# Output weight loaded ahead of the second chunk's v, first q norms as one-column matmuls, first A^T W in landing order

## Chip, core, metric

One core of one Trainium2 chip. The metric is the device time of one launch in microseconds (us). PE is the matmul engine, ACT the scalar and DVE the vector engine; POOL issues the loads. An eviction is the scaled copy of a result out of PSUM.

## The reference

```python
# q, k, v: (4, 6144, 256); w1, w2, w3: (256, 768); w_out: (768, 256)
qn = q / (norm(q, axis=1) + 1e-6);  kn = k / (norm(k, axis=1) + 1e-6)
a = softmax(kn^T @ qn / tau)              # per batch, 256 x 256
x = (v @ a).reshape(24576, 256)
h = max(max(x @ w1, x @ w2), x @ w3)      # 24576 x 768
out = h @ w_out
```

The kernel never forms x. It computes A^T-times-weight products (`aw`, 256 x 768, three of them) per batch and multiplies v by them, so that one 512-row chunk of v costs 36 h matmuls and 24 output products. A product below is a matmul of `aw`; `et` is the exponential of the softmax.

## The kernel before, where the change touches it

Loads run on one queue in this order: k, q (in pieces of 8, 8, 8, 8, 4, 4, 4, 2, 2 row groups), v of chunk 0, nine pieces of w, v of chunk 1. The output weight follows only after chunk 1's v is transposed.

```python
    load_v(0)
    for fp in range(d_ff // FT):
        load_w(fp)                       # w1, w2, w3, 256 columns each
    load_v(1)
    ...
    def gram(b):                         # first batch only
        ...                              # k.k, diagonal into dkm
        for tp in range(NG // 2):        # pairs of row groups, double-row fp8
            for j in range(CC):
                PE.matmul(ps[j][:, 0:C], lhsT=qt[:, tsl, jsl], rhs=kt[:, tsl, :], ...)          # q.k
                PE.matmul(ps[j][:, C:C + P], lhsT=qt[:, tsl, jsl], rhs=qt[:, tsl, jsl], ...)    # q.q
    def softmax_t(ps, rkb):
        for j in range(CC):              # the diagonal of q.q holds the squared norms
            DVE.tensor_tensor_reduce(out=scr, in0=ps[j][:, C:C + P], in1=ident, ..., accum_out=n2q[:, j:j + 1])
        ...                              # Ln, Exp, scaled exp into et
    def aw_first(et, aw):
        products(0, (0, 1)); sums(0); sums(1)
        DVE.reciprocal(out=rinv, in_=rs_ps[:, 0:CC])
        products(1, (0, 1))
        for j in range(CC):
            products(j, (2,))
        # then six evictions, ACT and DVE in turn, scaled by rinv
    ...
    # after chunk 1's v has been transposed:
    hold_loads(1)
    POOL.dma_start(out=wo_sb, in_=moe_w_out.rearrange("(fc p) d -> p fc d", p=P))
    load_v(2)
```

`h_block` computes one 128-row block of h for a chunk: two matmuls for each of the three weights, a copy of the first bank on ACT and two maxima on DVE. Six PSUM banks rotate under products and h matmuls, two under grams, transposes, row sums and outputs.

## Time and profile before

| | before |
|---|---|
| time, median of 4 runs | 573.33 us (573.17 to 573.77) |
| span of the profiled run | 571.9 us |
| PE busy | 97% |
| last q piece reaches PE | 33.87 us |
| first h matmul | 37.73 us |
| next products (end of the first h block) | 39.02 us |
| first output product | 51.07 us |

The lines are in the prediction below. Three things help to read them. A timeline line of several instructions gives the start of the first and the length up to the end of the last; a matmul's own length (0.27 for a 256-wide one) contains its drain, so the step between starts, not the length, is what it costs. The idle time in brackets is that of the engine just before. And a transfer in the chain of waits costs only what PE waited at its end.

### The profile page before, as it was taken

How to read it: one execution, taken by the hardware profiler on the slowest of the kernel's cores; microseconds unless marked ns; L12 is line 12 of the kernel's file. 1: busy time of each engine (PE TensorE's matmuls, PEld its weight loads, DVE VectorE, ACT ScalarE, POOL GpSimd, SP SyncE). 2: the span in 40 equal slices, each digit the busy share in tenths (PEclk: the TensorE clock that was granted, in tenths of full speed). 3: DMA queues.
4: the chain of work that ended last, by engine and by line, in shares of the span. 5: the costliest groups of instructions: out<-in, count | busy, mean ns of one | idle time of the engine just before them, and what ended most of it. 6: DMA issues, size and time to landing. Idle time of an engine off the chain costs nothing.

```text
span 571.9 us, 9438 instructions
## 1 busy us (share of the span) xinstructions
PE 552.9 (97%) x3344; PEld 329.1 (58%) x3344; DVE 415.9 (73%) x658; ACT 309.1 (54%) x540; POOL 233.3 (41%) x237
## 2 busy tenths in 40 slices
PE   3799999999999999999999999999999999999997
PEld 2665555555755555555575555555575555555566
DVE  0048777777887777777767777777768778778775
ACT  1044567767464576776535467767635444444443
POOL 2442357776460078776560048777750000000000
PEclk9999999999999999999999999999999999999999
DMA  9997999895479268975279339985437333132112
GB/s 143 106 147 121 132 238 138 158 133 107 111 83 171 70 109 157 135 149 107 57 133 149 97 79 141 147 143 99 122 81 160 75 77 108 56 104 64 56 55 76
DMA packets 76960, 65.64 MB, mean 115 GB/s; under 512 B 52464, under 2 KB 62576, under 8 KB 76784
## 3 DMA queue, kind: packets, MB, share of 16 engines
q0 software_dynamic: 19072, 26.48, 39.1%
q1 hardware_dynamic: 57696, 38.41, 24.1%
q8 instruction: 26, 0.43, 0.3%
q14 instruction: 22, 0.18, 0.1%
q10 hardware_dynamic: 144, 0.13, 0.1%
HBM read 78.64 MB, written 25.17 MB: 182 GB/s over the span
## 4 chain that ended last, share of the span: by engine, by line
PE 90%; DMA 6%; issue 2%; POOL 1%; DVE 0%; POOLq 0%
PE h_ps L378 64%; PE o_ps L398 22%; DMA v_sb<-in_v_dram 3%; PE gram L249 3%; PE ew_ps L300 2%; DMA q_sb<-in_q_dram 1%; DMA wo_sb<-in_moe_w_out_dram 1%; DMA vt_sb<-v_sb 1%; POOL k_sb L99 0%; PE o_ps L423 0%; POOL w_sb L135 0%; POOL q_sb L102 0%; DVE o_sb L450 0%; POOL ident masks.py:199 0%; PE rs_ps L288 0%
## 5 line engine op out<-in xcount | busy, mean ns | idle before, releaser
L378 PE MATMUL h_ps<-vt_sb,aw_sb 128*128 128x512 bf16 (+1 forms) x1764 | 406.6, 375 | 0.1
L378 PEld LDWEIGHTS <-aw_sb 128*128 128x128 bf16 x1764 | 171.7, 98 | 161.7 <-DVE aw_sb L306 2.4
L383 DVE TENSOR_TENSOR s_mx<-h_ps,s_mx 128x512 bf16<-128x512 f32 (+1 forms) x294 | 198.8, 676 | 82.2 <-ACT s_mx L382 82.0
L382 ACT ACTIVATE s_mx<-h_ps 128x512 bf16<-128x512 f32 (+1 forms) x294 | 172.3, 586 | 124.3 <-PE h_ps L378 123.4
L384 DVE TENSOR_TENSOR ht_sb<-h_ps,s_mx 128x512 bf16<-128x512 f32 (+1 forms) x294 | 200.2, 681 | 30.6
L208 POOL TENSOR_TENSOR acc<-acc,sq 128x768 f32<-128x768 f32 x88 | 144.3, 1649 | 69.3 <-ACT sq L200 53.1
L398 PE MATMUL o_ps<-wo_sb,ht_sb 128*128 128x256 bf16 x1128 | 153.8, 273 | 0.1
L398 PEld LDWEIGHTS <-ht_sb 128*128 128x128 bf16 x1128 | 110.4, 98 | 52.2 <-issue 0.3
L401 ACT ACTIVATE o_sb<-o_ps 128x512 f32<-128x512 f32 x94 | 56.1, 597 | 83.9 <-PE o_ps L398 83.9
L110 POOL DMA_DIRECT2D v_sb<-in_v_dram x48 | 27.8, 584 | 37.4 <-DMA vt_sb<-v_sb 35.2
L200 ACT ACTIVATE sq<-q_sb 128x768 bf16<-128x768 fp8e4 x48 | 40.5, 844 | 0.0
L200 ACT ACTIVATE sq<-k_sb 128x768 bf16<-128x768 fp8e4 x48 | 40.1, 835 | 0.0
L205 POOL CAST acc<-sq 128x768 f32<-128x768 bf16 x6 | 4.9, 821 | 65.7 <-ACT sq L200 65.7
L102 POOL DMA_DIRECT2D q_sb<-in_q_dram x33 | 18.4, 565 | 4.1 <-DMA v_sb<-in_v_dram 3.1
L168 PE MATMUL kk<-k_sb 128*128 128x256 fp8e4 x48 | 7.5, 338 | 12.3 <-DVE k_sb L154 6.5
L99 POOL DMA_DIRECT2D k_sb<-in_k_dram x29 | 16.1, 557 | 2.9 <-issue 1.1
L249 PE MATMUL gram<-k_sb,q_sb 128*128 128x512 fp8e4 x144 | 16.8, 276 | 0.0
L249 PEld LDWEIGHTS <-q_sb 128*128 128x256 fp8e4 x144 | 15.9, 136 | 0.6
L303 ACT ACTIVATE aw_sb<-ew_ps,rinv 128x384 bf16<-128x384 f32 (+1 forms) x24 | 13.1, 554 | 5.7 <-PE ew_ps L300 4.8
L221 POOL PARTITION_ALL_REDUCE tot<-acc x6 | 10.9, 1858 | 11.9 <-DVE s_mx L383 6.0
L300 PE MATMUL ew_ps<-w_sb,et 128*128 128x384 bf16 (+1 forms) x96 | 15.6, 313 | 0.0
L168 PEld LDWEIGHTS <-k_sb 128*128 128x256 fp8e4 x48 | 6.4, 182 | 13.2 <-DMA k_sb<-in_k_dram 6.7
(64 smaller groups left out, 116.5 us busy)
## 6 DMA issues: line engine op xcount, KB each, us to landing
out_dram<-o_sb SPq DMA_DIRECT2D x41, 512.0 KB, 2.9
v_sb<-in_v_dram POOLq DMA_DIRECT2D x48, 256.0 KB, 4.4
k_sb<-in_k_dram POOLq DMA_DIRECT2D x24, 192.0 KB, 5.9
q_sb<-in_q_dram POOLq DMA_DIRECT2D x24, 192.0 KB, 7.3
out_dram<-o_sb SPq DMA_DIRECT2D x13, 256.0 KB, 2.0
k_sb<-in_k_dram POOLq DMA_DIRECT2D x5, 256.0 KB, 11.2
w_sb<-in_moe_w_dram POOLq DMA_DIRECT2D x9, 128.0 KB, 5.7
kf<-in_k_dram SPq DMA_DIRECT2D x1, 1024.0 KB, 5.0
```

Source lines behind the costliest of these rows:

```text
L102: POOL.dma_start(out=qk[b][0][:, g0:g0 + w, :], in_=q_r[b][:, g0:g0 + w, :])
L110: POOL.dma_start(out=t, in_=v_r[gi // NCH, gi % NCH])
L200: ACT.activation(out=sq, in_=src, func=AF.Square)
L208: POOL.tensor_tensor(out=acc, in0=acc, in1=sq, op=ALU.add)
L249: PE.matmul(g[:, j * C:(j + 1) * C], lhsT=qt[:, tsl, j * P:(j + 1) * P], rhs=kt[:, tsl, :], start=(tp == 0 and j == 0), stop=(tp == NG // ...
L300: PE.matmul(ew[:, :w], lhsT=et[:, j, ic * P:(ic + 1) * P], rhs=w_sb[m][:, j, fsl], start=(j == 0), stop=(j == CC - 1))
L378: PE.matmul(t.rearrange("p (t n) -> p t n", n=P), lhsT=aw[m][:, ic, fsl], rhs=vt[:, tsl, ic, :], start=(ic == 0), stop=(ic == CC - 1))
L382: ACT.activation(out=s_mx, in_=hp[0], func=AF.Copy)
L383: DVE.tensor_tensor(out=s_mx, in0=hp[1], in1=s_mx, op=ALU.max)
L384: DVE.tensor_tensor(out=ht, in0=hp[2], in1=s_mx, op=ALU.max)
L398: PE.matmul(st["ps"][:, half], lhsT=ht[:, fc, t * P:(t + 1) * P], rhs=wo_sb[:, fc, :], start=(fc == 0), stop=(fc == FC - 1))
L401: ACT.activation(out=st["o"][:, t - 1:t + 1, :].rearrange("p t d -> p (t d)"), in_=st["ps"], func=AF.Copy)
```

## The change

Three parts, all in the first 52 us. The output weight's load goes ahead of chunk 1's v, so that the first output product need not wait. The q norms of the first batch come from squares on ACT and DVE, summed over partitions by matmuls against a column of ones, instead of q.q matmuls and diagonal reductions. The first products follow the landing order of the weights, with each row sum ahead of them; the third weight's products move into the first h block; the transposed v of chunk 0 goes to two banks, six of its eight blocks to be copied by DVE and two by ACT, where each copied four.

```diff
     for fp in range(d_ff // FT):
         load_w(fp)
+    wo_sb = consts.tile([P, FC, d_model], BF16, name="wo_sb")
+    POOL.dma_start(out=wo_sb, in_=moe_w_out.rearrange("(fc p) d -> p fc d", p=P))
     load_v(1)
 ...
+        def squares(g0, w):
+            ACT.activation(out=a[:, 0:h, :], in_=ra, func=AF.Square)
+            DVE.tensor_tensor(out=d[:, 0:h, :], in0=rd, in1=rd, op=ALU.mult)
+        def columns(rows, first=False, last=False):
+            for n, (t, r) in enumerate(rows):
+                for j in range(CC):
+                    PE.matmul(nq[:, j:j + 1], lhsT=t[:, r, j * P:(j + 1) * P], rhs=ones_c, ...)
 ...
-        products(0, (0, 1))
+        weight(0)
         sums(0)
+        products(0, 0)
         sums(1)
         DVE.reciprocal(out=rinv, in_=rs_ps[:, 0:CC])
-        products(1, (0, 1))
+        products(1, 0)
+        weight(1)
         for j in range(CC):
-            products(j, (2,))
+            products(j, 1)
 ...
+        def third(between):
+            weight(2)
+            for j in range(CC):
+                products(j, 2)
+            evacuate(2 * CC + 1, DVE)
+            between()
+            evacuate(2 * CC, ACT)
 ...
+    def h_block_first(aw, third):
+        matmuls(0, range(CC))
+        third(lambda: ACT.activation(out=s_mx, in_=hp[0], func=AF.Copy))
+        matmuls(1, range(CC))
+        matmuls(2, reversed(range(CC)))
 ...
-    for i in range(6):
-        PE.matmul(warm_ps, lhsT=ident, rhs=warm, start=(i == 0), stop=(i == 5))
+    for i in range(2):
+        PE.matmul(warm_ps, lhsT=ident, rhs=warm, start=(i == 0), stop=(i == 1))
```

More of the change, by code (lines that the diff above doesn't have):

```diff
@@ L75 @@
     sq_pool = ctx.enter_context(tc.tile_pool(name="sq", bufs=4))
+    sqq_pool = ctx.enter_context(tc.tile_pool(name="sqq", bufs=3))
     sm = ctx.enter_context(tc.tile_pool(name="sm", bufs=2))
@@ L118 @@
     SP.dma_start(out=kf, in_=k_r[0][:, 0:HEAD, :])
-    for load, widths in ((load_k, [8] * 5), (load_q, [8] * 4 + [4, 4, 4, 2, 2])):
+    QW = [8] * 4 + [4, 4, 4, 2, 2]
+    for load, widths in ((load_k, [8] * 5), (load_q, QW)):
         g0 = HEAD if load is load_k else 0
@@ L139 @@
         load_w(fp)
+    wo_sb = consts.tile([P, FC, d_model], BF16, name="wo_sb")
+    POOL.dma_start(out=wo_sb, in_=moe_w_out.rearrange("(fc p) d -> p fc d", p=P))
     load_v(1)
-    wo_sb = consts.tile([P, FC, d_model], BF16, name="wo_sb")
     ACT.preload_act_table_set("natural_log_exp_and_others")
@@ L157, with gram_first @@
     neg_ln_tau = -math.log(float(tau)) if float(tau) != 1.0 else 0.0
-    def gram(b):
-        qt, kt = qk[b]
+    def gram_first():
+        qt, kt = qk[0]
         kk = htile("kk")
@@ L173, in gram @@
             DVE.tensor_tensor(out=dkm[:, jsl], in0=kk[:, jsl], in1=ident, op=ALU.mult)
-        ps = [xtile(f"gram{j}") for j in range(CC)]
-        for tp in range(NG // 2):
-            tsl = slice(2 * tp, 2 * tp + 2)
-            last = tp == NG // 2 - 1
-            for j in range(CC):
-                jsl = slice(j * P, (j + 1) * P)
-                PE.matmul(ps[j][:, 0:C], lhsT=qt[:, tsl, jsl], rhs=kt[:, tsl, :],
-                          start=(tp == 0), stop=last, perf_mode=DR, skip_group_check=True)
-                PE.matmul(ps[j][:, C:C + P], lhsT=qt[:, tsl, jsl], rhs=qt[:, tsl, jsl],
-                          start=False, stop=last, perf_mode=DR, skip_group_check=True)
-            if tp == 11:
+        g = xtile("gram")
+        nq = htile("nq")
+        def squares(g0, w):
+            h = w // 2
+            a = sqq_pool.tile([P, QW[0] // 2, C], BF16, name="sqa")
+            d = sqq_pool.tile([P, QW[0] // 2, C], BF16, name="sqd")
+            ra, rd = qt[:, g0:g0 + h, :], qt[:, g0 + h:g0 + w, :]
+            ACT.activation(out=a[:, 0:h, :], in_=ra, func=AF.Square)
+            DVE.tensor_tensor(out=d[:, 0:h, :], in0=rd, in1=rd, op=ALU.mult)
+            return [(t, r) for t in (a, d) for r in range(h)]
+        def columns(rows, first=False, last=False):
+            for n, (t, r) in enumerate(rows):
+                for j in range(CC):
+                    PE.matmul(nq[:, j:j + 1], lhsT=t[:, r, j * P:(j + 1) * P], rhs=ones_c,
+                              start=(first and n == 0 and j == 0), stop=(last and n == len(rows) - 1),
+                              skip_group_check=True)
+        g0 = 0
+        rows = None
+        for i, w in enumerate(QW):
+            if rows:
+                columns(rows, first=(i == 1))
+            for tp in range(g0 // 2, (g0 + w) // 2):
+                tsl = slice(2 * tp, 2 * tp + 2)
+                for j in range(CC):
+                    PE.matmul(g[:, j * C:(j + 1) * C], lhsT=qt[:, tsl, j * P:(j + 1) * P], rhs=kt[:, tsl, :],
+                              start=(tp == 0 and j == 0), stop=(tp == NG // 2 - 1), perf_mode=DR,
+                              skip_group_check=True)
+            rows = squares(g0, w)
+            g0 += w
+            if i == 2:
                 kb_ps = htile("kb_ps")
@@ L190, in gram @@
                 ACT.activation(out=rkb, in_=lnk, func=AF.Exp, scale=-0.5)
-        return ps, rkb
+        columns(rows, last=True)
+        return [g[:, j * C:(j + 1) * C] for j in range(CC)], rkb, nq[:, 0:CC]
     SQW = 3
@@ L265, in exp_t, with softmax_first @@
         return et
-    def softmax_t(ps, rkb):
-        n2q = sm.tile([P, CC], FP32, name="n2q")
-        scr = sm.tile([P, P], FP32, name="scr")
-        for j in range(CC):
-            DVE.tensor_tensor_reduce(out=scr, in0=ps[j][:, C:C + P], in1=ident, scale=1.0, scalar=0.0,
-                                     op0=ALU.mult, op1=ALU.add, accum_out=n2q[:, j:j + 1])
+    def softmax_first(gs, rkb, n2q):
         lnq = sm.tile([P, CC], FP32, name="lnq")
@@ L276, in softmax_t @@
         ACT.activation(out=rq, in_=lnq, func=AF.Exp, scale=-0.5, bias=neg_ln_tau)
-        return exp_t(scaled([ps[j][:, 0:C] for j in range(CC)], rkb), rq)
+        return exp_t(scaled(gs, rkb), rq)
     def alloc_aw():
@@ L313, in aw_first, with weight @@
         rs_ps = xtile("rs_ps")
-        parts = [(m, ic, htile("ew_ps")) for m in range(3) for ic in range(CC)]
+        parts = []
+        def weight(m):
+            parts.extend((m, ic, htile("ew_ps")) for ic in range(CC))
         def sums(j):
@@ L319, in sums, with products, evacuate @@
                           start=(ic == 0 and j == 0), stop=(j == CC - 1), skip_group_check=True)
-        def products(j, ms):
+        def products(j, of):
             for m, ic, ew in parts:
-                if m in ms:
+                if m == of:
                     PE.matmul(ew[:, :FT], lhsT=et[:, j, ic * P:(ic + 1) * P], rhs=w_sb[m][:, j, 0:FT],
                               start=(j == 0), stop=(j == CC - 1))
-        products(0, (0, 1))
+        def evacuate(n, engine):
+            m, ic, ew = parts[n]
+            dst, src, r = aw[m][:, ic, 0:FT], ew[:, :FT], rinv[:, ic:ic + 1]
+            if engine is ACT:
+                ACT.activation(out=dst, in_=src, func=AF.Copy, scale=r)
+            else:
+                DVE.tensor_scalar_mul(out=dst, in0=src, scalar1=r)
+        weight(0)
         sums(0)
+        products(0, 0)
         sums(1)
         DVE.reciprocal(out=rinv, in_=rs_ps[:, 0:CC])
-        products(1, (0, 1))
+        products(1, 0)
+        weight(1)
         for j in range(CC):
-            products(j, (2,))
-        for n, (m, ic, ew) in enumerate(parts):
-            if n % 2 == 0:
-                ACT.activation(out=aw[m][:, ic, 0:FT], in_=ew[:, :FT], func=AF.Copy, scale=rinv[:, ic:ic + 1])
-            else:
-                DVE.tensor_scalar_mul(out=aw[m][:, ic, 0:FT], in0=ew[:, :FT], scalar1=rinv[:, ic:ic + 1])
-        return rinv
+            products(j, 1)
+        for m in range(2):
+            evacuate(CC * m, ACT)
+            evacuate(CC * m + 1, DVE)
+        def third(between):
+            weight(2)
+            for j in range(CC):
+                products(j, 2)
+            evacuate(2 * CC + 1, DVE)
+            between()
+            evacuate(2 * CC, ACT)
+        return rinv, third
     vts = {}
@@ L358, in v_transpose_pe @@
         vt = vt_tile(gi)
-        vt_ps = xtile("vt_ps", cols=TPC * C, dtype=BF16)
-        for i in range(TPC * CC):
-            PE.matmul(vt_ps[:, i * P:(i + 1) * P], lhsT=v_sb[:, i * P:(i + 1) * P], rhs=ident,
-                      is_transpose=True, start=(i == 0), stop=(i == CC * TPC - 1))
-        half = TPC * CC // 2
-        ps = vt_ps.rearrange("p (i n) -> p i n", n=P)
-        DVE.tensor_copy(out=vt[:, half:, :], in_=ps[:, half:, :])
-        ACT.activation(out=vt[:, :half, :], in_=ps[:, :half, :], func=AF.Copy)
+        n = TPC * CC
+        cut = 6
+        banks = [xtile("vt_ps", cols=TPC * C, dtype=BF16), ps_h.tile([P, TPC * C], BF16, tag="h", name="vt_ps2")]
+        for b, (lo, hi) in enumerate(((0, cut), (cut, n))):
+            for i in range(lo, hi):
+                PE.matmul(banks[b][:, i * P:(i + 1) * P], lhsT=v_sb[:, i * P:(i + 1) * P], rhs=ident,
+                          is_transpose=True, start=(i == lo), stop=(i == hi - 1))
+        pa, pb = (t.rearrange("p (i n) -> p i n", n=P) for t in banks)
+        DVE.tensor_copy(out=vt[:, 0:cut, :], in_=pa[:, 0:cut, :])
+        ACT.activation(out=vt[:, cut:n, :], in_=pb[:, cut:n, :], func=AF.Copy)
     def h_block(gi, aw, fc, tsl=slice(0, TPC)):
@@ L382, in h_block, with matmuls @@
         ACT.activation(out=s_mx, in_=hp[0], func=AF.Copy)
+        DVE.tensor_tensor(out=s_mx, in0=hp[1], in1=s_mx, op=ALU.max)
+        DVE.tensor_tensor(out=ht, in0=hp[2], in1=s_mx, op=ALU.max)
+    def h_block_first(aw, third):
+        vt = vts[0]
+        hp = []
+        def matmuls(m, ics):
+            t = htile(f"h_ps{m}")
+            for n, ic in enumerate(ics):
+                PE.matmul(t.rearrange("p (t n) -> p t n", n=P), lhsT=aw[m][:, ic, 0:P], rhs=vt[:, :, ic, :],
+                          start=(n == 0), stop=(n == CC - 1))
+            hp.append(t)
+        s_mx = mx_pool.tile([P, CHUNK], BF16, name="s_mx")
+        ht = hts[0][:, 0, :]
+        matmuls(0, range(CC))
+        third(lambda: ACT.activation(out=s_mx, in_=hp[0], func=AF.Copy))
+        matmuls(1, range(CC))
+        matmuls(2, reversed(range(CC)))
         DVE.tensor_tensor(out=s_mx, in0=hp[1], in1=s_mx, op=ALU.max)
@@ L452, in last_chunk @@
         SP.dma_start(out=dst[:, HT + 1, :], in_=o_sb[:, HT + 1, :])
-    ps = gram(0)
+    first = gram_first()
     warm_ps = htile("warm_ps")
-    for i in range(6):
-        PE.matmul(warm_ps, lhsT=ident, rhs=warm, start=(i == 0), stop=(i == 5))
-    et = softmax_t(*ps)
+    for i in range(2):
+        PE.matmul(warm_ps, lhsT=ident, rhs=warm, start=(i == 0), stop=(i == 1))
+    et = softmax_first(*first)
     v_transpose_pe(0)
     aw = alloc_aw()
-    rinv = aw_first(et, aw)
+    rinv, third = aw_first(et, aw)
     v_transpose(1)
@@ L471 @@
     hold_loads(1)
-    POOL.dma_start(out=wo_sb, in_=moe_w_out.rearrange("(fc p) d -> p fc d", p=P))
     load_v(2)
@@ L532 @@
             for fc in range(FC):
-                h_block(gi, aw, fc)
+                if gi == 0 and fc == 0:
+                    h_block_first(aw, third)
+                else:
+                    h_block(gi, aw, fc)
                 for f in gaps[fc]:
```

## The prediction

> **What bounds the kernel now.** I read the page's busy shares and slices first, then the chain of waits, then the timeline of the first 52 us, because all three parts of the change lie there.
>
> ```profile
> PE 552.9 (97%) x3344; PEld 329.1 (58%) x3344; DVE 415.9 (73%) x658; ACT 309.1 (54%) x540; POOL 233.3 (41%) x237
> PE   3799999999999999999999999999999999999997
> PE 90%; DMA 6%; issue 2%; POOL 1%; DVE 0%; POOLq 0%
> ```
>
> PE is full in every slice but the first two and the last. So a change in the head pays only by the amount by which the dense stream of matmuls starts earlier, or by holes that it fills. The chain of waits, cut to 0 to 75 us (start, length, what):
>
> ```profile
> 16.32 7.09 DMA q_sb<-in_q_dram
> 23.69 11.37 DMA v_sb<-in_v_dram
> 36.74 5.64 DMA v_sb<-in_v_dram
> 42.39 2.89 DMA vt_sb<-v_sb
> 45.57 5.45 DMA wo_sb<-in_moe_w_out_dram
> 51.07 0.82 PE o_ps L398 x6
> ```
>
> Read back, the first output product waits for the output weight, whose load was issued only at 45.57, after the second chunk's v was loaded and transposed. But the chain overstates that load: 5.45 us of it run beside dense PE work. How long PE itself waited comes from the timeline (start, length, engine, line, instruction, idle before):
>
> ```profile
> 33.87 0.32 PE L180 MATMUL gram<-k_sb,q_sb 128*128 128x512 fp8e4 x1 [0.15 <-DMA q_sb<-in_q_dram]
> 34.26 1.47 PE L458 MATMUL warm_ps<-warm,ident 128*128 128x512 bf16 x6
> 34.29 0.29 DVE L271 CUSTOM_DVE_ANT_0 scr<-gram,ident 128x128 f32<-128x128 f32 x1 [13.89 <-PE gram L182]
> 35.07 0.20 ACT L275 ACTIVATE lnq<-n2q 128x2 f32<-128x2 f32 x1 [6.22 <-DVE n2q L271]
> 35.54 0.91 ACT L264 ACTIVATE et<-e_in,rq 128x256 bf16<-128x256 f32 x2
> 35.56 0.61 PE L361 MATMUL vt_ps<-ident,v_sb 128*128 128x128 bf16 x8
> 36.10 0.70 PE L324 MATMUL ew_ps<-w_sb,et 128*128 128x256 bf16 x4
> 36.63 0.24 PE L318 MATMUL rs_ps<-ones_c,et 128*128 128x1 bf16 x4
> 36.67 0.60 ACT L366 ACTIVATE vt_sb<-vt_ps 128x512 bf16<-128x512 bf16 x1 [0.23 <-DVE vt_sb L365]
> 37.18 1.20 ACT L336 ACTIVATE aw_sb<-ew_ps,rinv 128x256 bf16<-128x256 f32 x3
> 37.73 1.46 PE L378 MATMUL h_ps<-vt_sb,aw_sb 128*128 128x512 bf16 x6
> 39.02 1.47 PE L300 MATMUL ew_ps<-w_sb,et 128*128 128x256 bf16 x12
> ...
> 44.37 6.63 PE L378 MATMUL h_ps<-vt_sb,aw_sb 128*128 128x512 bf16 x30
> ```
>
> Until 33.87 the load of q sets the pace. Then comes the chain of the first softmax (reduce, Ln, Exp, scaled exp), and from 36.10, when the first half of et is there, PE is nearly dense. Check: six h matmuls take 1.29 us in the chain, so 0.216 each; a 256-wide product takes 0.109 ((1.47 - 0.27)/11). From 36.10 up to the first output product the work is 36 products (3.92), 4 row sums (0.10) and 48 h matmuls (10.37), together 14.39 us. The 30 h matmuls from 44.37 run out at 44.37 + 30 x 0.216 = 50.85; the output product starts at 51.07. So PE lost 0.22 us to the output weight, and 50.85 - 36.10 - 14.39 = 0.36 us in small holes. That is all the slack there is after 36.10. The rest of any gain has to come from starting before 36.10.
>
> **What the Trainium skill says.** (1) "TensorE: Matmul & The Clock Gate", section "Wait — 56ns, not 53.3ns?": starts of small matmuls are never closer than about 25 ns. The trace agrees: four 1-column row sums take 0.24 us, that is 0.165 for one and three steps of 0.025. (2) Same page, "Part 1: The HAM clock gate": PE begins at half rate and is released by about 3.4 us of sustained work. The trace agrees in kind: in the gram stage the starts of a q.k and a q.q matmul lay 0.32 us apart from 21.0 on and 0.168 from 24.9 on, after 3.9 us without a hole. The k stage before it, busy 1.25 of each 2.45 us, never got the faster clock. (3) "PSUM — Partial Sum Buffer", "Terms": two engines may not use the same bank and quadrant at once. The 0.23 us that ACT's copy of vt waits for DVE's copy of the same bank agrees. (4) "SBUF — State Buffer", "SBUF: two separate sides": a DVE instruction with two SBUF inputs contends with a GpSimd instruction that reads SBUF. The new squares on DVE are such; nothing in this trace shows whether they hold up the issue of loads.
>
> **The change part by part.**
>
> *Norms as columns.* Removed: 48 q.q matmuls, two DVE diagonal reductions and four of the six warm-up matmuls. Added: for each of nine pieces of q a square on ACT and one on DVE, and 96 one-column matmuls (96 x 0.025 = 2.4 us, against 48 x 0.056 = 2.7 removed). Up to the last piece all this is beside the load: a piece of 8 groups comes every 2.45 us and costs at full clock 8 x 0.109 + 16 x 0.025 = 1.27 us of PE, and about 1.1 to 1.2 us on ACT and DVE (estimate from ACT's 768-wide squares at 0.84: about 0.2 fixed plus 0.8 ns per element). On the path lies the last piece alone. Before: 33.87 to Ln at 35.07. After: q seen by ACT and DVE at 33.88, a 256-wide square each about 0.42 (a 256-wide activation took 0.42, and a 256-wide DVE multiply about the same), hand-over 0.06, three steps of 0.025 plus 0.165 for the columns, hand-over 0.05: Ln at 34.65. The scaled exp follows Ln by 0.47 as before, at 35.12: gain 0.42 us. DVE's e_in multiplies start at about 34.36 and their first is done in time at 34.78.
>
> *But the next inputs don't come earlier.* The first v landed at 23.69 + 11.37 = 35.06, so transposes run 35.11 to 35.56. By issue plus time to landing the first three weight pieces came at 26.18 + 9.5 = 35.7, 28.61 + 7.8 = 36.4 and 29.87 + 7.2 = 37.1. New order: row sum of half 0 at 35.69, two products at 35.75 to 35.97, row sum of half 1 when the second exp is done at 36.03, so at 36.09, reciprocal 36.32 to 36.49 (before: 36.91 to 37.08), two products to 36.36, then four with the second weight from 36.42 to 36.86. The evictions start at 36.58 (before 37.18). Splitting vt over two banks takes ACT's copy out of their way: ACT 35.97 to 36.35, DVE 35.66 to 36.2.
>
> *First h block.* Its first matmul comes at 36.58 + 0.47 + 0.07 = 37.12 against 37.73, but with 8 products done where before all 12 were, and PE idle for 0.26. Two h matmuls to 37.56, four products with the third weight to 37.99, two h matmuls to 38.42. The third weight's ic1 is evicted by DVE only after its last product ends at 38.15: 38.20 to 38.68. Its ic0 comes on ACT after the 0.60 copy of the first h bank (37.76 to 38.36), at about 38.75. So PE waits 0.33, and the last two matmuls run 38.75 to 39.18. Before, the block's end (start of the next products) was 39.02. **So this part arrives about 0.16 us later than before**: the start gained 0.6, and the third weight, moved behind an eviction, gives it all back.
>
> *Output weight.* In the old trace the last weight piece landed at 36.0 + 5.1 = 41.1 and the queue then ran dry. The output weight is three pieces' worth of bytes; pieces landed 0.68 apart, so 2.0 us: landed at 43.1, v of chunk 1 at 44.4 instead of 42.38, and transposed 2.9 later at 47.3. Chunk 1's first h matmul was at 50.85 - 12 x 0.216 = 48.26, so it still holds with 1 us to spare. Gain: 0.22 us.
>
> Sum: +0.16 - 0.22 = -0.06 us, with 0.36 us of small holes that may move either way. Everything after about 52 us has the same instructions in the same order.
>
> **The rivals.** *The third weight comes free*: if DVE and ACT hand over faster than I reckoned, or the hole at 38.42 closes, the block ends by 38.7 and the whole saves 0.5 to 0.6: 572.7. For it: the reciprocal does come 0.6 earlier. Against: PE is in order, and the last product to the last h matmul is a chain of eviction latencies (0.47 each in the trace). *The clock is not released in time*: the gram stage now streams less; at half clock a piece takes 8 x 0.213 = 1.7 plus columns of 0.4 to 0.8, up to 2.5 of 2.45 us, with columns of hardly any array activity. If the release waits until chunk 0, about 3.4 us of work run at half rate: 1.7 to 3 us lost, 575 to 576. For it: the k stage at half load stayed slow. Against: the new stage is 85 to 100% occupied. I give it one in ten. *Chunk 1's v takes the place of the output weight*: if it lands over 1 us later than reckoned, PE waits before chunk 1, and the 0.22 is lost or turned around: 573.3 to 574. *Squares on DVE delay the issue of loads*: each load is issued 5 us or more before it lands, so a delay of 1 us is hidden.
>
> **Range and chances.** The working gives 573.2. The holes and the first rival pull down more than the third pulls up, so I say 573.0 us. The range is 572.2 (everything on the good side, about 1 us) to 574.4 (half of the clock's loss). Two per cent is 11.5 us, more than the whole head after the last q could give, so within 2% is all but sure: faster 0.01, same 0.98, slower 0.01.
>
> **What would show it.** Right: Ln of q about 0.4 us earlier; reciprocal near 36.5; first h matmul near 37.1; then a hole of 0.3 us ahead of the third weight's h matmuls; next products near 39.2; no hole ahead of the first output product; transposed v of chunk 1 near 47.3; the same spacing from chunk 1 on. Wrong: gram matmuls still 0.21 us apart after 30 us (clock), a hole ahead of chunk 1 (v), weight pieces landing later than 35.7, 36.4 and 37.1 (issue), or the first h block ending before 38.8.

## The result

| | before | after |
|---|---|---|
| time, median of 4 runs | 573.33 us (573.17 to 573.77) | 573.50 us (573.31 to 573.68) |
| span of the profiled run | 571.9 us | 571.9 us |

The ratio, the mean of one kernel's fast runs over the mean of the other's of the same rounds (so not quite the ratio of the medians), is 1.0002, with a 95% interval of 0.9984 to 1.0019: the same. The runs of one kernel scatter by 0.4 to 0.6 us, more than any net effect below. So the times can say no more than "same", and everything finer has to come from the traces. The two profiled executions took the same 573.68 us, so the 0.17 between the medians isn't in the traces.

The page of the changed kernel: busy share, and the chain by engine.

```profile
PE 552.8 (97%) x3387; PEld 327.7 (57%) x3388; DVE 423.3 (74%) x663; ACT 315.9 (55%) x549; POOL 233.2 (41%) x237
PE 93%; DMA 5%; POOL 0%; DVE 0%; issue 0%; ACT 0%; ACTq 0%; DVEq 0%; POOLq 0%
```

PE's busy time is the same; DVE and ACT took on some 7 us each of squares. The output weight has left the chain, which now follows the load of q, the squares, and from then on PE's own work. The chain's shares have moved by 3% of the span, and the time has not: a share of a chain is no gain.

The timeline of the changed kernel from the last q piece to the first h matmul:

```profile
33.91 0.43 PE L204 MATMUL gram<-k_sb,q_sb 128*128 128x512 fp8e4 x2
33.97 0.42 ACT L185 ACTIVATE sqa<-q_sb 128x256 bf16<-128x256 fp8e4 x1 [0.32 <-DMA q_sb<-in_q_dram]
33.99 0.42 DVE L186 TENSOR_TENSOR sqd<-q_sb 128x256 bf16<-128x256 fp8e4 x1 [0.30 <-DMA q_sb<-in_q_dram]
34.45 0.20 PE L192 MATMUL nq<-ones_c,sqa 128*128 128x1 bf16 x2
34.73 0.17 ACT L296 ACTIVATE lnq<-nq 128x2 f32<-128x2 f32 x1 [0.34 <-PE nq L192]
...
35.14 0.62 PE L406 MATMUL vt_ps<-ident,v_sb 128*128 128x128 bf16 x8
35.17 0.91 ACT L290 ACTIVATE et<-e_in,rq 128x256 bf16<-128x256 f32 x2
...
35.69 0.56 DVE L409 COPY vt_sb<-vt_ps 128x768 bf16<-128x768 bf16 x1 [0.48 <-PE vt_ps L406]
...
35.99 0.36 ACT L410 ACTIVATE vt_sb<-vt_ps 128x256 bf16<-128x256 bf16 x1
...
36.37 0.17 DVE L364 RECIPROCAL rinv<-rs_ps 128x2 f32<-128x2 f32 x1
36.64 0.84 ACT L356 ACTIVATE aw_sb<-ew_ps,rinv 128x256 bf16<-128x256 f32 x2 [0.29 <-PE ew_ps L349]
```

Ln comes at 34.73 instead of 35.07, the scaled exp at 35.17 instead of 35.54, the reciprocal at 36.37 instead of 36.91, the first eviction at 36.64 instead of 37.18. The two copies of vt now overlap (DVE from 35.69 to 36.25, ACT from 35.99 to 36.35). Each piece of the chain does what it was made for. Then the first h block of the changed kernel:

```profile
37.17 0.60 PE L438 MATMUL h_ps<-vt_sb,aw_sb 128*128 128x512 bf16 x2
...
37.61 0.60 PE L349 MATMUL ew_ps<-w_sb,et 128*128 128x256 bf16 x4
...
38.05 1.35 PE L438 MATMUL h_ps<-vt_sb,aw_sb 128*128 128x512 bf16 x4
38.25 0.48 DVE L358 TENSOR_SCALAR aw_sb<-ew_ps,rinv 128x256 bf16<-128x256 f32 x1 [0.69 <-PE ew_ps L349]
...
38.78 0.13 PEld L438 LDWEIGHTS <-aw_sb 128*128 128x128 bf16 x2 [0.64 <-DVE aw_sb L358]
...
39.23 1.47 PE L321 MATMUL ew_ps<-w_sb,et 128*128 128x256 bf16 x12
```

The first h matmul is 0.56 us earlier than before (37.17 against 37.73), and the products after the block are 0.21 us later (39.23 against 39.02). The reader sees why in the last weight load: it waited for the third weight's eviction on DVE, which itself ran only from 38.25, because its product stood at 37.61. Four h matmuls in one stretch would take 3 x 0.216 + 0.38 = 1.03; they took 1.35, so PE stood still for 0.32. Ahead of the first h matmul it stood still for about 0.3 as well (the last of the earlier products started at 36.76, and one costs 0.109).

The third weight was not late. By issue and time to landing in the table of transfers the first three weight pieces landed at 25.85 + 9.9 = 35.75, 28.27 + 8.1 = 36.37 and 30.34 + 6.7 = 37.04. Its products could have started 0.57 us earlier. That is at the end of the gap in which PE waited for the first eviction (about 36.87 to 37.17), so only some 0.1 us of this gap could have been filled. The four products cost 0.44 and would have moved the first h matmul to about 37.5; what their place costs, by this reckoning, is the hole of 0.32 behind it. The kernel before has them ahead of the first h matmul, and there the block runs without a hole: 39.02 - 37.73 = 1.29, six steps of 0.215.

At last the stretch to the first output product:

```profile
44.51 6.63 PE L422 MATMUL h_ps<-vt_sb,aw_sb 128*128 128x512 bf16 x30
...
47.43 0.19 POOL L534 COPY guard<-vt_sb 128x1 bf16<-128x1 bf16 x1 [9.22 <-DMA vt_sb<-v_sb]
...
50.98 0.82 PE L463 MATMUL o_ps<-wo_sb,ht_sb 128*128 128x256 bf16 x6
```

The 30 h matmuls run out at 44.51 + 30 x 0.216 = 50.99, and the output product starts there: the hole of 0.22 us is closed. The copy that waits for chunk 1's transposed v runs at 47.43 instead of 45.35, before chunk 1's first h matmul at 44.51 + 18 x 0.216 = 48.40 (18 of the 30 still belong to chunk 0), so v did not become the new wait. From the h matmuls after the third group of products (44.51 against 44.37) to the output product the two kernels have the same PE instructions, 6.47 us in one and 6.70 in the other.

Summed over the head, in differences after minus before: last q piece +0.04, scaled exp -0.37, first h matmul -0.56, next products +0.21, second group of h matmuls +0.14 (the second group of products lasts 1.31 instead of 1.38, so one small hole of 0.07 is gone), first output product -0.08.

That 0.08 us is carried on unchanged through 500 us, and is gone in the last chunk but one. Timeline lines of DVE and PE there, before:

```profile
554.52 0.69 DVE L383 TENSOR_TENSOR s_mx<-h_ps,s_mx 128x512 bf16<-128x512 f32 x1 [0.52 <-ACT s_mx L382]
...
555.32 0.69 DVE L384 TENSOR_TENSOR ht_sb<-h_ps,s_mx 128x512 bf16<-128x512 f32 x1
...
555.81 0.82 PE L398 MATMUL o_ps<-wo_sb,ht_sb 128*128 128x256 bf16 x6
```

and after:

```profile
554.45 0.69 DVE L427 TENSOR_TENSOR s_mx<-h_ps,s_mx 128x512 bf16<-128x512 f32 x1 [0.52 <-ACT s_mx L426]
...
555.60 0.69 DVE L428 TENSOR_TENSOR ht_sb<-h_ps,s_mx 128x512 bf16<-128x512 f32 x1 [0.46 <-PE h_ps L422]
555.74 0.89 PE L463 MATMUL o_ps<-wo_sb,ht_sb 128*128 128x256 bf16 x6
...
556.35 0.10 PEld L463 LDWEIGHTS <-ht_sb 128*128 128x128 bf16 x1 [0.18 <-DVE ht_sb L428]
```

The same DVE maximum starts 1.15 us after the one ahead of it in the changed kernel and 0.80 in the one before. The profile names PE, but PE was 0.07 earlier than before, not later. The late maximum ends at 555.60 + 0.69 = 556.29, and the weight load of the sixth output product waits for it (last line). So the group of output products is stretched by 0.07, and from the next h matmul on (556.47 in both) the kernels stand at the same time.

The pause is no single event. Each h block ends with two maxima on DVE. Of the 294 second maxima of the changed kernel seven start with an idle time of 0.46 to 0.52 where all others have 0.10 to 0.11: at 49.76, 104.31, 216.26, 271.30, 443.86, 499.80 and 555.60. In the kernel before, none of 294 does. Counted along all of DVE's records in the packed trace, its waits for semaphores included, the seven are numbers 64, 192, 448, 576, 960, 1088 and 1216: each is 64 more than a multiple of 128. The three other such places up to there (320, 704 and 832) hold no second maximum. In the kernel before these places hold other records (nine of ten times a wait for a semaphore), and from 52 us on PE's instructions are the same in both. The changed kernel has 11 more DVE records, all in the head. So the pause goes with a place in DVE's sequence, and the change, as far as one trace of each kernel can show it, moved maxima onto such places. Six of the seven cost PE nothing; the one at 555.60 cost the 0.07. What DVE does at these places isn't shown, and no run tested it.

### The profile page after: what moved, and what is told of

The parts are those of the page before. It is cut to its first block, busy times and chain, and to the rows that moved or that the text cites. A ratio compares the mean times of both kernels' runs of the same rounds, so it can differ in the third digit from the quotient of the medians.

```text
span 571.9 us, 9549 instructions
## 1 busy us (share of the span) xinstructions
PE 552.8 (97%) x3387; PEld 327.7 (57%) x3388; DVE 423.3 (74%) x663; ACT 315.9 (55%) x549; POOL 233.2 (41%) x237
## 4 chain that ended last, share of the span: by engine, by line
PE 93%; DMA 5%; POOL 0%; DVE 0%; issue 0%; ACT 0%; ACTq 0%; DVEq 0%; POOLq 0%
PE h_ps L422 65%; PE o_ps L463 22%; DMA q_sb<-in_q_dram 5%; PE gram L275 3%; PE ew_ps L321 3%; POOL k_sb L100 0%; PE o_ps L488 0%; PE h_ps L438 0%; DVE aw_sb L358 0%; PE ew_ps L349 0%; PE vt_ps L406 0%; DVE ht_sb L428 0%; DVE o_sb L515 0%; ACT sqa L185 0%; PE warm_ps L523 0%
## 5 line engine op out<-in xcount | busy, mean ns | idle before, releaser
L185 ACT ACTIVATE sqa<-q_sb 128x1024 bf16<-128x1024 fp8e4 (+2 forms) x9 | 7.0, 772 | 19.3 <-DMA q_sb<-in_q_dram 19.3
```

## The experiments

No experiment gave a result, so what follows tells what was meant and what it leaves open. Four kernels were handed over first. All four were turned away before a chip ran them, because at that time no matmul performance mode was admitted, and both kernels compute their grams with the fp8 double-row mode. These are their edits and what was expected of them, on record before.

*Output weight alone*: the kernel before, with one move.

```diff
     for fp in range(d_ff // FT):
         load_w(fp)
+    wo_sb = consts.tile([P, FC, d_model], BF16, name="wo_sb")
+    POOL.dma_start(out=wo_sb, in_=moe_w_out.rearrange("(fc p) d -> p fc d", p=P))
     load_v(1)
-    wo_sb = consts.tile([P, FC, d_model], BF16, name="wo_sb")
 ...
-    POOL.dma_start(out=wo_sb, in_=moe_w_out.rearrange("(fc p) d -> p fc d", p=P))
```

> The kernel before with the output weight's load moved ahead of chunk 1's v, nothing else. Theory (the move only fills the hole ahead of the first output product): the next products after the first h block start at 39.0 as before, the first output product at 50.84 to 50.87 instead of 51.07, no hole in front of it, transposed v of chunk 1 at about 47.3. Rival (v takes the output weight's place as the wait): a hole ahead of chunk 1's first h matmul near 48.2 and the first output product at 51.0 or later. Time within 0.1% of before in either case.

*Columns alone*: the kernel before with the new gram and softmax of the first batch.

```diff
-    ps = gram(0)
-    for i in range(6):
+    first = gram_first()
+    for i in range(2):
 ...
-    et = softmax_t(*ps)
+    et = softmax_first(*first)
```

> The kernel before with the first q norms as columns of squares (and two warm-up matmuls), the old order of products and row sums, the old single bank of vt, the old place of the output weight. Theory (an earlier exp is of no use as long as the products stand ahead of the row sums, because they wait for the second weight, landed at about 36.4): scaled exp at about 35.2 instead of 35.54, but reciprocal at 36.85 to 36.95 as before, first h matmul at 37.65 to 37.75 as before, next products within 0.1 of 39.02. Rival (the softmax chain sets the block's end): everything up to the next products comes 0.35 us earlier, about 38.65.

*Landing order alone*: the changed kernel with the two other parts undone.

```diff
-    first = gram_first()
+    ps = gram(0)
 ...
-    et = softmax_first(*first)
+    et = softmax_t(*ps)
 ...
-    POOL.dma_start(out=wo_sb, ...)   # back behind hold_loads(1)
```

> The changed kernel without the columns (old gram with diagonal reductions, six warm-up matmuls) and without the move of the output weight: only the landing order of the first products, the two banks of vt and the third weight inside the first h block. Theory (this part has a hole of about 0.33 us of its own and follows the exp): scaled exp at 35.54, first h matmul at about 37.5, next products at about 39.55 to 39.65, that is 0.5 later than before, the output product's hole shrinks because the weight stays where it was, first output product within 0.1 of 51.2. Rival (the landing of the weights sets the pace, not the exp): next products at 39.2 to 39.3 as in the changed kernel.

*Third weight early*: the changed kernel with the third weight's products ahead of the first h matmul, which is also the version that might beat both.

```diff
-        matmuls(0, range(CC))
-        third(lambda: ACT.activation(out=s_mx, in_=hp[0], func=AF.Copy))
+        third(lambda: None)
+        matmuls(0, range(CC))
+        ACT.activation(out=s_mx, in_=hp[0], func=AF.Copy)
         matmuls(1, range(CC))
-        matmuls(2, reversed(range(CC)))
+        matmuls(2, range(CC))
```

> The changed kernel with the third weight's products and evictions put ahead of the first h matmul, ACT's copy of the first h bank after them. Theory (the hole ahead of the last two h matmuls is the chain product, DVE eviction, behind the third weight's late place): no hole inside the first h block, next products at about 38.85 instead of 39.23, first output product at about 50.6 instead of 50.98, unless the release of a bank by DVE's second maximum (about 40.3) stops the sixth pair of the next products, which would give back up to 0.35. Rival (the third weight lands too late to be used earlier): PE stands still ahead of the first h matmul until after 37.4 and the block ends at 39.1 to 39.3.

*Stand-ins without the mode.* So that the head could still be measured, four stand-ins were made (of both kernels, of the output weight alone and of the third weight early): each double-row gram matmul was replaced by one ordinary matmul over the first of its two row groups: the same output width, a wrong result, and, so it was hoped, the same timing.

```diff
-            tsl = slice(2 * tp, 2 * tp + 2)
+            tsl = 2 * tp
 ...
-                          stop=(tp == NG // 2 - 1), perf_mode=DR, skip_group_check=True)
+                          stop=(tp == NG // 2 - 1), skip_group_check=True)
```

They build. They were handed over eight times in about two hours, in sets of one to four, 20 kernels in all, but each time no chip ran them. What was expected of the stand-in of the kernel before:

> Stand-in for the kernel before, without a matmul performance mode: each double-row gram matmul over two row groups is replaced by one ordinary matmul of the same output over the first of the two groups (wrong result on purpose; norms and grams see half of the rows). It should keep the timing of the original: gram stage paced by the load of q, last q piece at about 33.85, q.k and q.q starts 0.166 apart at full clock, scaled exp at 35.54, first h matmul at 37.73, next products at 39.02, first output product at 51.07 with a hole of about 0.22 in front, each within 0.1. If landmarks differ by more than 0.2 the stand-ins tell nothing of the originals, only of each other. Time within 0.3% of before.

What that leaves open. The part of each edit is read from one trace of each kernel, not measured by undoing it. That the third weight's place causes the hole of 0.32 us is argued from the order of instructions, the named wait and the block without a hole in the kernel before; that moving it forward would end the block at about 38.85 and bring the whole some 0.4 us ahead of the changed kernel is an estimate, from the same steps as the prediction. Whether the columns alone or the landing order alone would gain anything isn't known. What the two traces do show by themselves is that the hole ahead of the output product is gone, in a stretch in which PE has the same instructions in both.

## Why the prediction was right, point by point

- *Only the head can pay.* Right: from 52 us to 554 us the two kernels stay 0.08 us apart.
- *Norms as columns, gain 0.42 at the exp.* Nearly: 0.37. The squares took 0.42 each as reckoned, but started 0.09 to 0.11 later than I had them, since the last q piece came 0.04 later and ACT and DVE started 0.06 to 0.08 after PE instead of with it. Counted from the last q piece the gain is (35.54 - 33.87) - (35.17 - 33.91) = 0.41. The way from the squares to Ln was as reckoned (34.73 - 33.97 = 0.76, said 0.77); the exp followed Ln by 0.44 instead of 0.47, which hides part of the late start.
- *The next inputs don't come earlier.* Right: transposes at 35.14 (said 35.11), products at 35.80 (35.75), second weight's products between 36.4 and 36.9. The reciprocal came at 36.37 (36.32).
- *First h matmul near 37.12, a hole of 0.33 behind, next products 39.18.* Right: 37.17, 0.32, 39.23, each 0.05 late, most of it from the last q piece (0.04). The gain of 0.56 at the first h matmul is turned into a loss of 0.21. The sum said +0.16 from a last q piece at the old time; taken from the last q piece on it is 39.23 - 33.91 - (39.02 - 33.87) = 0.17.
- *Output weight, gain 0.22, v not the new wait.* Right: hole closed, transposed v of chunk 1 used at 47.43. One clause of the working is wrong, though not its sum: the queue did not run dry behind the last weight piece, since chunk 1's v, 256 KB, still followed and landed at 42.38.
- *Sum -0.06.* The trace has -0.08 at the first output product. That it comes so near is in part luck: the block ended 0.05 later than the sum has it, and one of the small holes that the sum left open closed by 0.07.
- *Clock rival.* It did not come. Gram stage of the changed kernel, PE lines of the timeline from 20 to 26 us:

```profile
20.66 1.97 PE L204 MATMUL gram<-k_sb,q_sb 128*128 128x512 fp8e4 x8 [1.19 <-DMA q_sb<-in_q_dram]
22.42 0.42 PE L192 MATMUL nq<-ones_c,sqa 128*128 128x1 bf16 x8
22.70 0.35 PE L192 MATMUL nq<-ones_c,sqd 128*128 128x1 bf16 x8
23.12 1.65 PE L204 MATMUL gram<-k_sb,q_sb 128*128 128x512 fp8e4 x8
...
25.61 0.65 PE L204 MATMUL gram<-k_sb,q_sb 128*128 128x512 fp8e4 x4 [0.44 <-DMA q_sb<-in_q_dram]
```

  The first eight take (1.97 - 0.42) / 7 = 0.22 a step, the eight from 23.12 on average 0.20 (1.38 in all: taken one by one in the trace, their starts lie 0.21 apart up to 24.24, then 0.15, then 0.11), and those from 25.61 on (0.65 - 0.27) / 3 = 0.13, the first of them slower. So the full clock came within the second piece, at about 24.3, some 3.6 to 3.7 us after the stage began, and no later than in the kernel before (24.9, after 3.9). In this trace the 16 one-column matmuls in between did not put it off.
- *Loads delayed by squares on DVE.* It did not come: the three weight pieces landed at 35.75, 36.37 and 37.04, where 35.7, 36.4 and 37.1 were expected.
- *The number.* The working gave 573.2 (0.06 less than 573.29, the median of the first three runs of the kernel before) and I said 573.0, because I let the favourable rival pull. The measured 573.5 lies 0.17 above before, with both medians inside the scatter of the other's runs; the pull toward the good side was the part of the prediction with no step behind it. Where the 0.08 that the trace still had at 51 us went, the DVE pause at 555 us, was in no step either: the prediction took it that the same instructions in the same order would carry the gain to the end. The range from 572.2 to 574.4 is far wider than the 0.06 that was reckoned, so that the time fell into it tests none of the steps; the landmarks in the trace do.

## What to carry to other kernels

A chain that is shortened at its head helps only down to the next thing that PE waits for. Here 0.56 us won in front of the first h matmul were spent again, because the third weight's products were placed behind it, so that their own eviction came to lie on the path. When an order follows the landing of loads, compare the landing times with the times at which the engine really gets there: a piece that has landed before the engine's wait is over may belong in front of what the engine waits to do (argued here, not tested). And before a load is moved to free a chain of waits, count how long the engine really stood at its end: 5.45 us in the chain were 0.22 us of PE.

## What the Trainium skill lacked or had wrong

- "TensorE: Matmul & The Clock Gate", section "Wait — 56ns, not 53.3ns?": the floor of about 25 ns between starts of small matmuls is given with an example at the fast clock alone. At half clock it is hardly higher: eight one-column matmuls at 22.70 take 0.35 us, (0.35 - 0.165) / 7 = 0.026 a step, against three steps of 0.025 for the row sums at full clock. The page's N ÷ 1.2 GHz between starts at the slow clock, called exact there, can hold only above that floor: for one column it would give 0.001 us.
- Same page, "Part 1: The HAM clock gate": it doesn't say how busy a window must be, or whether matmuls with one column count. Here PE at 1.25 of each 2.45 us stayed at half clock in the k stage, and a stage of eight gram matmuls and sixteen one-column ones, with some 0.23 us between the last of these and the next gram matmul, was released 3.6 to 3.7 us after it began.
- "SBUF — State Buffer", "Who interferes with whom": it tells that a DVE instruction with two SBUF inputs contends with GpSimd instructions that read SBUF, and infers that the making of descriptors is not among them. The runs bear it out: each of the nine squares on DVE (0.42 to 1.23 us) ran beside the issue of a load, the issues of the first two weight pieces wholly inside one, and these took 0.73 and 0.72 us, as in the kernel before, where DVE stood still at that time.
- No page has it: in the trace of the changed kernel seven of 294 DVE maxima start some 0.36 to 0.42 us late, each at a record of DVE whose number is 64 more than a multiple of 128. At the one at 555.60 a PE matmul is named that had kept its step. What DVE waits for there stays open.
